# GpSimd gathers the random key columns of every tile but the first; the engine orders are rewritten

## The chip, the cores and the metric

The kernel runs on one core of one Trainium2 chip. The metric is device time in microseconds of one launch; the median of three runs of the kernel before is 801.58 us (798.22 to 808.25). Engines are named PE (TensorE, matmul), DVE (VectorE), ACT (ScalarE), POOL (GpSimd) and SP (the queue that issues most of the DMAs).

## The reference: block-sparse attention, then a cosine feed-forward

```python
B, H, S, D = 4, 8, 768, 64; block = 32          # 24 blocks of keys and of queries
scores = q @ k.transpose(0, 1, 3, 2) / sqrt(D)
mask = |blk_i - blk_j| <= 1, or blk_i or blk_j is the first or the last block
mask[qb, kb] = True for the 3 random kb in sampled_blocks[qb]   # the same for all batches and heads
attn = softmax(where(mask, scores, -1e9)) @ v
x = attn as (B * S, H * D) = (3072, 512)
h = x @ w_in                                     # 512 -> 2048
out = (h * cos(h)) @ w_out                       # 2048 -> 512
```

All inputs are float32. The kernel splits every operand of a matmul into two float16 parts, high and low, and multiplies three of the four pairs, so each product of the reference is three matmuls.

## The kernel before: 24 tiles, one table of places

The 3072 rows are 24 tiles of 128 query rows, six in each of the four batches. The first five of a batch (i = 0 to 4) are sparse: four query blocks each, whose keys are their neighbours, the first and the last block, and three random blocks for each query block. The sixth is dense under a mask. Two tiles make one block of the feed-forward, m0 to m11.

**Names of steps.** For a sparse tile n: wgd and wga gather its random key columns; qk{n}_0 to qk{n}_3 are the scores of two heads each; mx adds the mask and takes row maxima; ex exponentiates; ph and pl split the probabilities; PT turns them by a DMA; pv{n}_0 to pv{n}_3 multiply with the values; no, xh, xl and xT normalise, split and turn the rows for the feed-forward. A feed-forward block m has 16 up steps m{m}_p_c (12 matmuls each) and 16 down steps d{m}_p_t_h (6 matmuls each). vi{n}_0 to vi{n}_3 are indirect DMAs of POOL that fetch the random value rows of tile n. kT turns the keys of a batch into the buffer W, by DMA.

**The gather.** W holds a batch's keys with the key index in the free dimension. The 12 random blocks of a tile are copied into Wg, 8 heads of 32 columns for each copy, at offsets that stand in registers. There is one buffer Wg, so the gather of tile n + 1 can't start before the last score step of tile n has read it, and the first score step of tile n + 1 needs it. In batch 0, tiles 1 to 4 are gathered by POOL (wgp, line 1564, 12 copies). Tile 0 and all tiles of batches 1 to 3 are gathered by DVE (8 copies) and ACT (4 copies) side by side (line 1434), with a tile i = 0 of a later batch in two halves, as soon as each half of W is there. The registers are loaded by load_pool_regs on POOL (12 each for i = 1 to 4, at the start, line 1207) and by load_regs on DVE (8 each) and ACT (4 each) for i = 0 to 4 (line 1217); those of i = 1 to 4 come later, between other work.

**Other single buffers.** The scores of a step lie in sp, of which there is one: a score step waits until mx of the step before has read sp. V, the values of a tile, has two buffers, and POOL's vi steps of a tile wait for one to come free.

**The order.** All steps are named and listed once. The string PLACES gives each a place, and every engine runs its steps in the order of places; the costs in the code (the numbers after the engine in op(...)) only choose which buffer of a class a step takes. So the order on each engine, on SP's and POOL's queues too, is what PLACES says.

```python
    def k_gather(self, n, Wg, h0, h1, which):
...
            src = Wz[:, h0:h1, :, bass.ds(reg, BLK // 2)]
            dst = Wg[:, h0:h1, j, BLK * s : BLK * s + BLK].rearrange("p h (z c) -> p h z c", z=2)
            if which == 2:
                self.nc.gpsimd.tensor_copy(dst, src)
            else:
                self.copy(dst, src, which)
```

Of the kernel before, what the change touches and what calls it, by code (L numbers as in the profile page):

```python
# [45 lines left out]
    GP=[0, 1, 1, 1, 1],  # L46
# [37 lines left out]
wlm5 344 wlp5 345 wc11_2 346 wl14 347 wl15 348 xl0 349 mx2_3_0 350 mx2_3_1 351 pv1_0 352 pv1_2 353 PF2_0_1 354 nb2_3 355 wlp4 356 wc13_0 357 wc13_1
358 ph2_0_0 359 ph2_0_1 360 pl2_0_1 361 ex2_3_0 362 ph1_3_0 363 ex2_2_0 364 ph1_3_1 365 wgp3 366 qk3_0 367 mx3_0_0 368 mx3_0_1 369 qlo4 370 qk3_1 371
ql5 372 ql5#2 373 uT4 374 nb3_0 375 ex3_0_0 376 ex3_0_1 377 ph3_0 378 pl1_3_0 379 wlm7 380 wlp7 381 pl1_3_1 382 pl2_0_0 383 wc13_2 384 wsq13 385 wl16
386 wl17 387 pl3_0 388 mx3_1_0 389 mx3_1_1 390 nb3_1 391 wlm6 392 wc14_0 393 wc15_0 394 wc14_1 395 wc15_1 396 wc14_2 397 wl18 398 wc15_2 399 wl19 400
wlp6 401 PF2_1_0 402 PF2_1_1 403 pv1_1 404 qk3_2 405 mx3_2_0 406 mx3_2_1 407 PF2_2_0 408 PF2_2_1 409 pv1_3 410 no1 411 ex2_3_1 412 qsq5 413 vg4_0 414
vg4_1 415 vi4_0 416 vi4_2 417 vi4_3 418 ex3_1_0 419 wsq9 420 wsq11 421 wred8 422 ph2_1_0 423 pl2_1_0 424 ph2_1_1 425 ex3_1_1 426 ph3_1 427 wall8s 428
wall8 429 wsc8c 430 wsq15 431 wred12 432 wsc8e 433 nb3_2 434 ph2_2_0 435 pl2_2_0 436 ph2_2_1 437 XF1 438 xh1 439 qk3_3 440 pv2_0 441 wsc8s 442 whi8  # L90
443 wsi8 444 wlm8 445 wlm9 446 wlp8 447 wc17_0 448 qsc5c 449 whi10 450 rs2 451 PF2_3_1 452 mx3_3_0 453 mx3_3_1 454 pl2_1_1 455 pv2_1 456 qsc5e 457
pl2_2_1 458 pv2_2 459 wall12s 460 nb3_3 461 ex3_3_1 462 pl3_1 463 PT3_1 464 ex3_2_0 465 wlm10 466 wc17_1 467 wc17_2 468 wl20 469 wl21 470 vg4_2 471
wall12 472 PF2_3_0 473 wgp4 474 qk4_0 475 turn0_1 476 wsc12c 477 xl1 478 vi4_1 479 wsc12e 480 m0_0_0 481 m0_0_1 482 wc18_0 483 wc19_0 484 wc18_1 485
wlp9 486 qu5 487 wc19_1 488 PT3_0 489 ex3_3_0 490 ph2_3_0 491 ph2_3_1 492 pl2_3_1 493 wc19_2 494 wl23 495 mx4_0_0 496 wlp10 497 ph3_3 498 m0_0_2 499
m0_0_3 500 mx4_0_1 501 ex3_2_1 502 ph3_2 503 rs3 504 pl3_2 505 ev0_0_0 506 ev0_0_1 507 pl2_3_0 508 pv2_3 509 nb4_0 510 ex4_0_0 511 rr3 512 wc18_2 513
# [387 lines left out]
def plan_kernel(env, B, H, S, D, DM, DFF, pr):  # L483

    pl = Plan()
    e = env
    NB = S // BLK
    NT = S // P
# [62 lines left out]
    for which in range(2):  # L551
        for i in range(pr["RN"][which]):
            load_regs(i, which)
# [1495 lines left out]
```

## Time and profile before

| what | value |
|---|---|
| median of 3 runs | 801.58 us (798.22 to 808.25) |
| the profiled execution: its own time, its span | 804.44 us, 802.5 us |
| busy: PE, DVE, ACT, POOL | 730.0, 636.2, 624.3, 133.0 us |
| granted TensorE clock, mean over the span | 0.968 |
| chain that ended last, by engine | PE 50%, DVE 21%, DMA 10%, ACT 10% |

Busy time is the sum of an engine's instructions; a PE that is busy is not PE at its peak. The chain is followed back from the last instruction, at each step to what released it. The profiled execution's own time is 2.9 us above the median of the runs.

### The profile page before, as it was taken

Reading aid. Unit: us, or ns where it says so; the run is one execution under the profiler, and the core shown is the slowest. Engines: PE = TensorE matmul, PEld = TensorE weight load, DVE = VectorE, ACT = ScalarE, POOL = GpSimd, SP = SyncE. Lnnn points to the kernel's source line nnn. Section 1 sums busy time; section 2 is a strip of 40 time slices with the busy share of each in tenths; the row PEclk is TensorE's granted clock in tenths of the full one; section 3 lists DMA queues with packets and bytes.
Section 4 is the critical chain, followed back from the end, with each engine's and each line's share of the span. In section 5 each row is a group of like instructions: output and inputs, shape, how many; then the busy total and the mean of one; then the engine's idle time right before and its main releaser. Section 6 shows DMA issues by size and latency. Waiting matters only on the chain.

```text
span 802.5 us, 25057 instructions
## 1 busy us (share of the span) xinstructions
PE 730.0 (91%) x10288; PEld 486.7 (61%) x10288; DVE 636.2 (79%) x1576; ACT 624.3 (78%) x1202; POOL 133.0 (17%) x180
## 2 busy tenths in 40 slices
PE   3587799986999888999999999999799999999998
PEld 3445475654675546756666557677466577566763
DVE  4979999999789875988868988988588858876362
ACT  2578889897669986989969989898589976896242
POOL 1667440002100221001110223001202202000000
PEclk9679999998999979999999999999999999999999
DMA  9885798999746999999998899999848979664101
GB/s 240 275 251 150 219 230 199 202 201 228 179 95 117 173 187 175 192 228 224 182 184 148 167 216 212 180 196 227 187 71 159 156 137 173 155 136 92 28 1 52
DMA packets 295410, 136.97 MB, mean 171 GB/s; under 512 B 253952, under 2 KB 275584, under 8 KB 295296
## 3 DMA queue, kind: packets, MB, share of 16 engines
q1 hardware_dynamic: 290176, 119.65, 73.2%
q0 software_dynamic: 5120, 15.73, 8.4%
q8 instruction: 80, 1.31, 0.7%
q14 instruction: 34, 0.28, 0.1%
HBM read 68.23 MB, written 12.58 MB: 101 GB/s over the span
## 4 chain that ended last, share of the span: by engine, by line
PE 50%; DVE 21%; DMA 10%; ACT 10%; issue 5%; POOL 2%; SPq 1%; ACTq 0%; DVEq 0%; POOLq 0%
PE ph L1920 22%; PE ph L1970 17%; DVE P L1625 4%; DMA PT<-ring 4%; ACT P L1646 3%; DMA xT<-n 3%; DVE ring L1660 2%; PE sp L1590 2%; PE ph L1708 2%; DMA qs<-in_q_dram 2%; PE sp L1609 1%; PE ph L1724 1%; POOL Wg L1564 1%; ACT junk L1302 1%; PE ph L1696 1%
## 5 line engine op out<-in xcount | busy, mean ns | idle before, releaser
L1920 PE MATMUL ph<-xT,w 128*128 128x256 f16 x2304 | 269.6, 275 | 11.1 <-DMA xT<-n 11.1
L1970 PE MATMUL ph<-w,g 128*128 128x512 f16 x1152 | 266.3, 381 | 2.1 <-DVE ot L1747 1.1
L1920 PEld LDWEIGHTS <-w 128*128 128x128 f16 x2304 | 223.4, 99 | 48.2 <-DMA xT<-n 10.5
L1970 PEld LDWEIGHTS <-g 128*128 128x128 f16 x1152 | 107.6, 98 | 121.9 <-issue 6.0
L1549 POOL DMA_INDIRECT V<-scr,gidx x80 | 90.9, 1136 | 508.6 <-PE ph L1696 255.8
L1646 ACT ACTIVATE P<-P,sm 128x352 f32<-128x352 f32 (+1 forms) x224 | 152.1, 680 | 17.2 <-DVE sm L1640 14.8
L1625 DVE CUSTOM_DVE_ANT_1 P<-sp,bias 128x352 f32<-128x352 f32 x160 | 77.4, 518 | 31.5 <-PE sp L1595 26.1
L1660 DVE TENSOR_TENSOR ring<-P,ring 128x704 f16<-128x704 f32 (+1 forms) x100 | 90.2, 909 | 14.9 <-ACT ring L1656 14.7
L1929 ACT ACTIVATE hs<-ph,sm 128x512 f32<-128x512 f32 x96 | 63.0, 677 | 28.9 <-PE ph L1920 25.7
L1656 ACT CAST ring<-P 128x704 f16<-128x704 f32 (+1 forms) x100 | 78.6, 789 | 7.4 <-DMA PT<-ring 6.1
L1947 ACT ACTIVATE g<-g,sm 128x1024 f32<-128x1024 f32 x48 | 54.8, 1146 | 25.8 <-DVE g L1943 25.4
L1952 DVE SCALAR_TENSOR_TENSOR hs<-hs,sm,g 128x1024 f32<-128x1024 f32 x48 | 61.3, 1280 | 14.7 <-ACT g L1947 14.6
L1961 DVE TENSOR_TENSOR g<-hs,g 128x1024 f16<-128x1024 f32 x48 | 58.5, 1220 | 14.8 <-ACT g L1958 14.7
L1958 ACT ACTIVATE g<-hs 128x1024 f16<-128x1024 f32 x48 | 50.4, 1051 | 20.0 <-DVE hs L1952 17.7
L1943 DVE SCALAR_TENSOR_TENSOR g<-g,hs 128x1024 f32<-128x1024 f32 x48 | 58.7, 1224 | 1.2
L1939 DVE TENSOR_SCALAR g<-hs 128x1024 f32<-128x1024 f32 x48 | 33.0, 687 | 26.1 <-ACT hs L1929 26.0
L1590 PE MATMUL sp<-W,U 64*128 64x192 f16 x960 | 43.3, 226 | 11.0 <-DVE sm L1625 10.9
L1590 PEld LDWEIGHTS <-U 64*128 64x128 f16 x960 | 30.0, 98 | 33.2 <-issue 31.5
L1708 PE MATMUL ph<-V,PT 128*128 128x64 f16 x960 | 42.5, 195 | 0.0
L1646 ACT ACTIVATION_READ_ACCUMULATOR P<-P,sm 128x1 f32 x224 | 42.3, 189 | 0.0
L1625 DVE CUSTOM_DVE_ANT_1 P<-sp,dbias 128x384 f32<-128x384 f32 x64 | 33.1, 552 | 5.1 <-PE sp L1609 3.9
L1595 PE MATMUL sp<-Wg,U 64*32 64x96 f16 x1920 | 29.3, 212 | 8.3 <-POOL Wg L1564 4.2
(163 smaller groups left out, 868.0 us busy)
## 6 DMA issues: line engine op xcount, KB each, us to landing
V<-scr SPq DMA_DIRECT2D x20, 384.0 KB, 5.0
w<-in_moe_w_in_dram SPq DMA_DIRECT2D x12, 512.0 KB, 5.8
w<-in_moe_w_out_dram SPq DMA_DIRECT2D x12, 512.0 KB, 4.7
V<-scr SPq DMA_DIRECT2D x8, 768.0 KB, 5.6
scr<-n SPq DMA_DIRECT2D x21, 256.0 KB, 3.3
qs<-in_q_dram SPq DMA_DIRECT2D x20, 256.0 KB, 4.3
stage<-in_v_dram SPq DMA_DIRECT2D x9, 512.0 KB, 5.8
stage<-in_k_dram SPq DMA_DIRECT2D x9, 512.0 KB, 5.6
```

The lines of the kernel that those rows point to most:

```text
L1549: self.nc.gpsimd.indirect_dma_start(V[:96, 2 + j, :], None, self.scr[b][:, :], bass.IndirectOffsetOnAxis(ap=self.gidx[:96, c : c + 1], axi ...
L1590: mm(out, u[r], x, start=(first and not part), stop=False, tile_position=(a * D, 0))
L1625: self.nc.vector.tensor_tensor_reduce(out=self.p_view(n, Pt)[:, a].rearrange("p (n c) -> p n c", c=hf), in0=sp[:, :w].rearrange("p (n c) - ...
L1646: self.nc.scalar.activation(Pv[:, a], Pv[:, a], AF.Exp, scale=qc[:, 4:5], bias=nb[:, a : a + 1], accum_out=sums[:, x : x + 1],)
L1656: self.nc.scalar.copy(R[:, :, 0, : self.width(n)], self.p_view(n, Pt))
L1660: self.nc.vector.tensor_tensor(R[:, :, 1, :w], self.p_view(n, Pt), R[:, :, 0, :w], ALU.subtract)
L1708: mm(xp[:, h, :], PT[:, 6 * a + 3 * l + c, :], V[:, c, h, d0:d1], start=False, stop=(a == 1 and c == 1 and x == len(terms) - 1),)
L1920: self.nc.tensor.matmul(ph[:, ff, :], self.W1[p][:, wl, cc, c * P : (c + 1) * P], xT[:, xl * NCC + cc, :], start=(j == 0), stop=(j == len( ...
L1929: self.nc.scalar.activation(hs[:, h * 512 : h * 512 + 512], ph.rearrange("p f t -> p (f t)"), AF.Copy, scale=self.turns[b][:, p : p + 1])
L1943: self.nc.vector.scalar_tensor_tensor(kt, kt, MAGIC, hs, op0=ALU.subtract, op1=ALU.subtract)
L1952: self.nc.vector.scalar_tensor_tensor(hs, hs, c[:, p : p + 1], kt, op0=ALU.mult, op1=ALU.mult)
L1970: self.nc.tensor.matmul(self.flat32(po), g[:, gl, ff, t * P : (t + 1) * P], self.W2[p][:, wl, ff, :], start=(first and ff == half * hf and ...
```

## The change

POOL gathers the keys of all tiles but the first, in batches 1 to 3 too (12 copies for each tile, for i = 0 in two halves of 12). DVE and ACT gather tile 0 alone, and their register loads for i = 1 to 4 go. POOL loads the registers of i = 1 to 3 once at the start, as before; those of i = 0 and i = 4 it loads each time, in the instructions just ahead of the copies. The table PLACES is new as a whole, and a few costs in the code. The diff without the table:

```diff
-    for i in range(1, NS):
+    for i in range(1, NS - 1):
         if pr["GP"][i]:
             pregs[i] = Val()
             op("POOL", 3.2, pr["RG"][i], lambda i=i: e.load_pool_regs(i), r=[sx], w=[pregs[i]], name=f"pregs{i}")
     for which in range(2):
         for i in range(pr["RN"][which]):
-            load_regs(i, which)
+            if not pr["GP"][i]:
+                load_regs(i, which)
...
-        if i in pregs and not b:
+        if b:
+            for h0, h1 in [(0, HH), (HH, H)] if i == 0 else [(0, H)]:
...
+                cost = (7.1 if h1 - h0 == H else 5.1) + (0.0 if i in pregs else 3.2)
+                op("POOL", cost, pos + 0.01 * h0, lambda h0=h0, h1=h1: e.k_gather(n, Wg.t, h0, h1, 2), r=part + [pregs.get(i, sx)], w=keys, name=f"wgp{n}")
+            return
+        if pr["GP"][i] and not b:
...
-            op("POOL", 4.6, pos, lambda: e.k_gather(n, Wg.t, 0, H, 2), r=part + [pregs[i]], w=keys, name=f"wgp{n}")
+            op("POOL", 7.1 if i in pregs else 10.3, pos, lambda: e.k_gather(n, Wg.t, 0, H, 2), r=part + [pregs.get(i, sx)], w=keys, name=f"wgp{n}")
...
-        for k, reg in enumerate(self.pregs[i] if which == 2 else self.regs[i, which]):
+        for k, reg in enumerate(self.pool_regs(i) if which == 2 else self.regs[i, which]):
```

In the rows below, line numbers of the changed kernel are 11 higher than those of the kernel before from the changed register functions on (1564 becomes 1575).

On POOL's queue, around the gather of tile 1 (V_107 and V_108 are the two buffers V, the DMA rows are vi steps, and each copy has an ISA row ahead of it). Before:

```order
L1298 TENSOR_SCALAR dbias<-V_107 128x24
L1549 DMA V_107<-scr_124,gidx 96x1024 x4
L1564 ISA
L1564 COPY Wg_109<-W 128x8x32
...
L1549 DMA V_108<-scr_124,gidx 96x1024 x4
```

Now:

```order
L1309 TENSOR_SCALAR dbias<-V_107 128x24
L1560 DMA V_108<-scr_124,gidx 96x1024 x2
L1575 ISA
L1575 COPY Wg_109<-W 128x8x32
...
L1560 DMA V_108<-scr_124,gidx 96x1024 x2
L1560 DMA V_107<-scr_124,gidx 96x1024 x4
```

Two of tile 0's four value fetches have moved behind the copies of tile 1's gather.

On DVE, at the last maxima of tile 8 and the first of tile 9 (the two ISA rows on line 1625 are mx, L1660 is pl, L1961 is a step of the feed-forward). Before:

```order
L1625 ISA P_99,sm<-sp_117,bias 128x352
L1625 ISA sm 128x1
L1217 TENSOR_LOAD sx
L1625 ISA P_99,sm<-sp_117,bias 128x352
L1625 ISA sm 128x1
L1640 TENSOR_SCALAR sm<-sm 128x2
L1434 ISA
L1434 COPY Wg_109<-W 128x8x32
...
L1660 TENSOR_TENSOR ring_103<-P_98,ring_103 128x2x352
L1961 TENSOR_TENSOR g_85<-hs_84,g_85 128x1024
```

Now:

```order
L1636 ISA P_100,sm<-sp_117,bias 128x352
L1636 ISA sm 128x1
L1636 ISA P_100,sm<-sp_117,bias 128x352
L1636 ISA sm 128x1
L1963 SCALAR_TENSOR_TENSOR hs_83<-hs_83,sm,g_88 128x1024
L1671 TENSOR_TENSOR ring_103<-P_99,ring_103 128x2x352
L1518 TENSOR_SCALAR sm<-sm 128x1
L1651 TENSOR_SCALAR sm<-sm 128x2
L1972 TENSOR_TENSOR g_88<-hs_83,g_88 128x1024
```

The register load between the two maxima and the eight copies are gone.

On PE, from the last value step of tile 17 to the first up step of m8, which needs tile 17's turned rows (each row stands for a run of equal ones; L1970 are down steps, L1920 up steps). Before:

```order
L1724 MATMUL ph_118<-V_107,PT_106 128x64
...
L1970 MATMUL ph_122<-w_0_68,g_86 128x512
...
L1970 MATMUL ph_119<-w_0_68,g_86 128x512
...
L1970 MATMUL ph_119<-w_1_69,g_87 128x512
...
L1920 MATMUL ph_121<-xT_110,w_0_64 128x256
```

Now:

```order
L1735 MATMUL ph_122<-V_107,PT_104 128x64
...
L1931 MATMUL ph_123<-xT_111,w_3_67 128x256
...
L1981 MATMUL ph_120<-w_3_71,g_88 128x512
...
L1981 MATMUL ph_122<-w_0_68,g_86 128x512
...
L1931 MATMUL ph_119<-xT_110,w_0_64 128x256
```

Before there are five down steps between the two; now there are two up steps of m7 and seven down steps.

## Rows read from the trace of the kernel before

**Rows 1.** Busy time by stretch: stretch, us, engines, PE clock, DMA share, GB/s.

```profile
160.00:200.00 40.00, 29.54 (x317) 19.89 (x316) 39.55 (x74) 33.47 (x61) 4.62 (x4) 0.93 1.03 216
...
200.00:300.00 100.00, 93.03 (x1298) 59.84 (x1298) 83.44 (x235) 79.32 (x161) 14.24 (x12) 0.94 0.77 151
...
sum 602.50, PE 576.60 PEld 382.61 DVE 456.44 ACT 472.61 POOL 65.37; mean PE 96.10 PEld 63.77 DVE 76.07 ACT 78.77 POOL 10.90
```

**Rows 2.** Groups by line and shape: busy us, mean ns | idle before.

```profile
L1434 DVE COPY Wg<-W 128x256 f16 x104 | 15.4, 223 | 0.2 <-PE sp L1595 0.2
L1434 DVE COPY Wg<-W 128x128 f16 x48 | 5.7, 188 | 1.7 <-DMA W<-kn 1.7
L1434 ACT COPY Wg<-W 128x256 f16 x52 | 17.0, 399 | 0.0
L1434 ACT COPY Wg<-W 128x128 f16 x24 | 5.3, 290 | 1.0 <-DMA W<-kn 1.0
```

**Rows 3.** Register loads by line: duration ns min/median/max.

```profile
L1217 DVEq TENSOR_LOAD <-sx x5: 1847/2096/3264, 9.9 to 286.9; - x5
L1207 POOLq TENSOR_LOAD <-sx x4: 2722/2726/2931, 9.9 to 18.5; - x4
```

**Rows 4.** Timeline of POOL: start, us, [idle before <-releaser].

```profile
46.23 0.92 POOL L1549 DMA_INDIRECT V<-scr,gidx  x1 [0.30 <-DVE sm L1625]
47.16 5.24 POOL L1564 COPY Wg<-W 128x256 f16 x12
...
74.86 7.61 POOL L1564 COPY Wg<-W 128x256 f16 x12 [2.15 <-PE sp L1595]
```

**Rows 5.** The tile Wg: POOL's copies, ns min/median/max.

```profile
L1564 POOL COPY Wg<-W x48: 386/393/1466, 47.2 to 102.7; 128x256 f16 x48
```

**Rows 6.** Timeline of DVE.

```profile
52.83 0.52 DVE L1625 CUSTOM_DVE_ANT_1 P<-sp,bias 128x352 f32<-128x352 f32 x1 [3.18 <-PE sp L1595]
...
80.57 1.29 DVE L1804 SCALAR_TENSOR_TENSOR w<-w,w 128x1024 int32<-128x1024 int32 x1
...
289.96 0.52 DVE L1625 CUSTOM_DVE_ANT_1 P<-sp,bias 128x352 f32<-128x352 f32 x1 [2.56 <-issue]
```

**Rows 7.** Timeline of PE.

```profile
43.35 0.44 PE L1595 MATMUL sp<-Wg,U 64*32 64x96 f16 x24
...
279.45 0.64 PE L1590 MATMUL sp<-W,U 64*128 64x192 f16 x12 [1.71 <-DVE sm L1625]
...
307.31 2.96 PE L1920 MATMUL ph<-xT,w 128*128 128x256 f16 x13 [3.12 <-DMA xT<-n]
...
407.55 4.65 PE L1920 MATMUL ph<-xT,w 128*128 128x256 f16 x41 [0.68 <-DMA xT<-n]
...
573.97 3.21 PE L1920 MATMUL ph<-xT,w 128*128 128x256 f16 x16 [5.58 <-DMA xT<-n]
...
619.30 0.51 PE L1590 MATMUL sp<-W,U 64*128 64x192 f16 x12
619.74 0.32 PE L1595 MATMUL sp<-Wg,U 64*32 64x96 f16 x24
619.99 0.36 PE L1696 MATMUL ph<-V,PT 96*32 96x64 f16 x24
...
620.64 4.09 PE L1920 MATMUL ph<-xT,w 128*128 128x256 f16 x36
...
642.65 1.47 PE L1920 MATMUL ph<-xT,w 128*128 128x256 f16 x12 [1.74 <-DMA xT<-n]
```

**Rows 8.** The chain that ended last: start, us, what.

```profile
266.37 1.02 issue
...
287.40 2.56 issue
...
763.71 9.17 PE ph L1920 x84
...
778.07 20.73 PE ph L1970 x96
```

More of the change, by code (lines that the diff above doesn't have):

```diff
@@ new lines @@
+qlo12 1468 PT10_0 1469 vg10_1 1470 xT8 1471 st2_0 1472 ex11_0_0 1473 pv9_3 1474 kload2_0 1475 PT10_2 1476 no9 1477 st1_1 1478 ph10_3 1479 ex11_1_1
+1480 ka3_2 1481 d3_0_1_0 1482 d3_0_1_1 1483 d3_1_1_0 1484 d3_1_1_1 1485 xh9 1486 pl10_3 1487 vhi2_2 1488 uT12 1489 ex11_0_1 1490 ph11_0 1491 ev3_3_0
+1492 xl9 1493 qk11_3 1494 mx11_3_0 1495 xT9 1496 ex11_1_0 1497 ph11_1 1498 ev3_3_1 1499 kb3_2 1500 vg11_0 1501 pv10_0 1502 vhi2_3 1503 rs10 1504
+mx11_3_1 1505 nb11_3 1506 pl11_0 1507 ka3_3 1508 vlo2_2 1509 PT10_3 1510 ksq2_1 1511 vst2_2 1512 rr10 1513 vhi2_0 1514 vlo2_3 1515 kload2_2 1516
@@ new lines @@
+m5_1_1 1806 ev5_1_0 1807 qk12_3 1808 mx12_3_0 1809 mx12_3_1 1810 nb12_3 1811 m5_1_3 1812 ex12_2_1 1813 ph12_2 1814 ql17 1815 ql17#2 1816 st3_1 1817
+pl12_2 1818 PT12_2 1819 ph12_1 1820 pl12_1 1821 PT12_1 1822 vg13_2 1823 m5_2_2 1824 m5_2_1 1825 vsq3_5 1826 ev5_1_1 1827 ka5_1 1828 kb5_1 1829
+d5_0_0_0 1830 pv12_0 1831 vsq3_2 1832 d4_3_1_0 1833 uT14 1834 ex12_3_1 1835 ex12_3_0 1836 ph12_3 1837 rs12 1838 pl12_3 1839 rr12 1840 PT12_3 1841
+wgp13 1842 qk13_0 1843 mx13_0_0 1844 mx13_0_1 1845 nb13_0 1846 m5_2_3 1847 vsq3_3 1848 qsq17 1849 qsc17c 1850 qsc17e 1851 qsc17s 1852 qu17 1853 qnu17
@@ new lines @@
+ex16_0_1 2097 ex16_1_0 2098 nb16_2 2099 ph16_0 2100 m6_1_3 2101 m6_1_1 2102 qhi18 2103 qlo18 2104 ex16_1_1 2105 pl16_0 2106 m6_2_2 2107 sin6_0 2108
+gm6_0 2109 qk16_3 2110 mx16_3_0 2111 mx16_3_1 2112 nb16_3 2113 ev6_1_0 2114 ev6_1_1 2115 ka6_1 2116 kb6_1 2117 ql19 2118 pv15_3 2119 vg16_0 2120
+vg16_1 2121 vg16_2 2122 vi16_0 2123 vi16_1 2124 vi16_2 2125 vi16_3 2126 m6_2_0 2127 ph16_1 2128 pl16_1 2129 PT16_1 2130 qk17_0 2131 mx17_0_0 2132
+mx17_0_1 2133 gh6_0 2134 gl6_0 2135 pv15_1 2136 m6_2_1 2137 sin6_1 2138 gm6_1 2139 m6_2_3 2140 qk17_1 2141 mx17_1_0 2142 mx17_1_1 2143 nb17_1 2144
@@ new lines @@
+2964 mx23_7_0 2965 mx23_7_1 2966 nb23_7 2967 ex23_6_0 2968 ex23_6_1 2969 ex23_7_0 2970 ex23_7_1 2971 rs23 2972 rr23 2973 pv23_1 2974 pv23_2 2975
+ka10_1 2976 kb10_1 2977 sin10_0 2978 gm10_0 2979 PT23_5 2980 ph23_4 2981 pl23_4 2982 d9_3_0_0 2983 d9_3_0_1 2984 o9_0 2985 m10_2_0 2986 sin10_1 2987
+gm10_1 2988 ph23_6 2989 pl23_6 2990 m10_2_2 2991 ph23_7 2992 pl23_7 2993 gh10_0 2994 gl10_0 2995 m10_2_1 2996 ev10_2_0 2997 pv23_3 2998 m10_3_2 2999
+m10_3_3 3000 m10_2_3 3001 ev10_2_1 3002 ka10_2 3003 kb10_2 3004 d10_0_1_0 3005 gh10_1 3006 gl10_1 3007 PT23_4 3008 pv23_4 3009 d10_0_1_1 3010
@@ L309 @@
+3102 gh11_3 3103 gl11_3 3104 d11_1_0_0 3105 d11_1_1_0 3106 d11_1_1_1 3107 d11_2_1_0 3108 d11_2_1_1 3109 d11_1_0_1 3110 d11_2_0_0 3111 d11_3_1_0 3112
+d11_3_1_1 3113 o11_1 3114 st11_1 3115 st11_1#2 3116 d11_2_0_1 3117 d11_3_0_0 3118 d11_3_0_1 3119 o11_0 3120 st11_0 3121
 """
@@ L682, in prep_q @@
             tp = Val(pr["UC"])
-            op("PE", 0.58, pos, lambda: e.q_turn(qs.t, tp.t), r=[qs, wide], w=[tp], name=f"UF{n}")
+            op("PE", 0.7, pos, lambda: e.q_turn(qs.t, tp.t), r=[qs, wide], w=[tp], name=f"UF{n}")
             op("ACT", 0.613, pos, lambda: e.q_square(qc.t, qs.t, None), r=[qs], w=[am], name=f"qsq{n}")
@@ L729, in gather_k @@
         tiles[n]["Wg"] = Wg
-        if i in pregs and not b:
+        if b:
+            for h0, h1 in [(0, HH), (HH, H)] if i == 0 else [(0, H)]:
+                part = [(W, (h, t)) for h in range(2) if h0 <= h * HH < h1 for t in range(NT)]
+                keys = [(Wg, (x, h)) for x in "da" for h in range(2) if h0 <= h * HH < h1]
+                cost = (7.1 if h1 - h0 == H else 5.1) + (0.0 if i in pregs else 3.2)
+                op("POOL", cost, pos + 0.01 * h0, lambda h0=h0, h1=h1: e.k_gather(n, Wg.t, h0, h1, 2), r=part + [pregs.get(i, sx)], w=keys, name=f"wgp{n}")
+            return
+        if pr["GP"][i] and not b:
             part = [(W, (h, t)) for h in range(2) for t in range(NT)]
             keys = [(Wg, (x, h)) for x in "da" for h in range(2)]
-            op("POOL", 4.6, pos, lambda: e.k_gather(n, Wg.t, 0, H, 2), r=part + [pregs[i]], w=keys, name=f"wgp{n}")
+            op("POOL", 7.1 if i in pregs else 10.3, pos, lambda: e.k_gather(n, Wg.t, 0, H, 2), r=part + [pregs.get(i, sx)], w=keys, name=f"wgp{n}")
             return
@@ L1015, in plan_kernel @@
         for i in range(pr["RN"][which], NS):
-            load_regs(i, which, [by[("ksc0s", "ksq0_2")[which]]])
+            if not pr["GP"][i]:
+                load_regs(i, which, [by[("ksc0s", "ksq0_2")[which]]])
     load_v(0, pr["V0"])
@@ L1203, in const_regs, with pool_regs @@
         nc.vector.memset(self.halfpi, math.pi / 2)
-    def load_pool_regs(self, i):
+    def pool_regs(self, i):
+        if i in self.pregs:
+            return self.pregs[i]
         x = 3 * (1 + 4 * i)
-        self.pregs[i] = self.nc.values_load_multi_w_load_instructions(
+        return self.nc.values_load_multi_w_load_instructions(
             self.sx[0:1, x : x + 12],
@@ L1213, in load_pool_regs @@
         )[1]
+    def load_pool_regs(self, i):
+        self.pregs[i] = self.pool_regs(i)
     def load_regs(self, i, which):
```

479 lines of the change are left out of this document (229 added, 250 removed).

## The prediction

> **What bounds the kernel now.** I read the busy time by stretch first. From 200 us to the end PE is busy 576.6 of 602.5 us, so 25.9 us are left there, and a granted clock of 0.94 in the first of these stretches [rows 1] takes about 6 us more (6% of 100). Before 200 us DVE is the bound: 39.55 of 40 us in the stretch from 160 [rows 1]. DVE and ACT have room behind 200 us (456 and 473 of 602 us), so work taken from them there counts only where PE waits for them. Then I read the timeline of PE for its waits. The long ones behind 200 us are not for a gather: they are for turned rows (3.12, 0.68, 5.58 and 1.74 us) and for mx, which frees the single score buffer (1.71 us) [rows 7]. The chain adds two waits called issue, of 1.02 and 2.56 us, at 266 and 287 [rows 8]; there DVE loads registers between two maxima, and the second is the idle time before the maximum at 289.96 [rows 6, 8].
>
> A step's price on PE, from its pace: an up step 9.17 / 7 = 1.31 us, a down step 20.73 / 16 = 1.30 us [rows 8], a score step 0.69 us (619.30 to 619.99), of which the first 0.44 don't touch Wg, and a value step 0.65 us (to 620.64) [rows 7].
>
> **The change part by part.** Removed: 96 of the 104 full copies on DVE (15.4 x 96/104 = 14.2 us) and the 48 half ones (5.7 us), 48 of 52 and 24 on ACT (15.7 + 5.3 us) [rows 2], together 19.9 us of DVE and 21.0 us of ACT, and four register loads on each (2.1 us on DVE as a median [rows 3]).
>
> *What that gives back.* Nearly all of it lies where PE is the bound and other work covers it. The waits listed above take 12.8 of PE's 25.9 idle us, and not for these engines' gathers; of the rest, which is spread over many short waits, I take -1.0 (ends -3.0 and 0). The loads that end on the chain at 266 and 287 are worth up to 1.02 + 2.56 = 3.6 us [rows 8]; behind them the chain goes on to the turned rows that m3 waits for, so some of it may only lengthen that wait. I take -2.5 (ends -3.6 and 0).
>
> *POOL's gather, its length.* Twelve copies took 5.24 us at 47 us and 7.61 us at 75 us [rows 4]; a copy is 0.39 us as a median and 1.47 at the longest [rows 5]. The long one ran beside DVE operations with two operands in SBUF, such as the one of 1.29 us at 80.57 [rows 6]. The feed-forward has operations of that kind, so I take 6.9 us, nearer the upper end.
>
> *Does PE wait for it?* The new order puts more work on PE between the last score step of one tile and the first of the next. Counting steps in the two orders: before tiles 7, 8 and 9 it was 3.25, 3.9 and 3.25 us, now 5.88 (three up, one down, one value), 6.5 (four down, two value) and 5.85 us (three down, three value). Before tiles 13 to 15 and 19 to 22 it is now 7.15 to 11.1 us, and 10.5 to 11.1 for i = 4 (tiles 10, 16, 22), which also has a load of 2.72 us [rows 3] ahead of its copies. The need is the gather less about 0.4 us, for the part of a score step that doesn't touch Wg: 6.5 us, and 9.2 with the load. So tiles 7 and 9 wait 0.6 and 0.65 us and the others nothing: +1.3. With 5.24 us it is 0, with 7.61 us (need 7.2) 1.3 + 0.7 + 1.35 + 0.1 = +3.5.
>
> *First tiles of a batch.* Two halves, each with a load of 2.72 us and 12 copies of half the size. No such copy is in the trace; the half copy takes 188 for 223 ns on DVE and 290 for 399 on ACT [rows 2], so 3.8 to 5.2 us for twelve, against 0.9 us on DVE and ACT side by side (a sixth of 5.7 and 5.3). The new order has 2.6, 7.0 and 6.5 us more PE work between the maximum of a batch's keys and its first score step (22.2 for 19.6, 35.1 for 28.1, 27.6 for 21.1 us), which covers the difference in batches 2 and 3 and most of it in batch 1: 0, and at most +2 for each of the three batches, if the second half is late.
>
> *Packed scores.* With the work moved between the tiles, less is left between the scores of one tile. In tiles 7 to 9 three pairs of score steps now stand with nothing between them, where it was one pair; that one waited 1.71 us for mx [rows 7]. Two more such waits are 3.4 us; the old order also lost time to mx elsewhere in these tiles, for which I take off one such wait: +1.7 (ends +1.0 and +2.6).
>
> *POOL's queue at the start.* Tile 0's last score step ended at 43.8 us [rows 7], but POOL was still issuing vi until 47.15 and only then gathered tile 1 [rows 4]; DVE sat idle 3.18 us before 52.83 for the scores behind it [rows 6], in the one part where DVE has idle time ahead of the stretch that it bounds. With two vi behind the copies the gather can start up to 3.3 us earlier. The moved vi must land before tile 0's values are multiplied, several us later. The vlo steps that POOL waits for ahead of its first vi now stand behind the first maxima, which gives back a part: -2.5 (ends -3.3 and 0). The four scores of tile 0 are packed too, +-2 around zero. The load of i = 4 that leaves the start had no one waiting.
>
> *Turned rows.* PE work between a tile pair's last value step and the first up step: for m5 10.4 us, now 7.8; m6 12.6, now 8.2; m8 6.5, now 11.7; m9 7.2, now 6.6; m3 7.4, now 8.7; m11 9.1, now 7.8; the rest hardly change or have more. What was needed is the old work plus the wait [rows 7]: m5 11.1, m8 12.1, m9 8.9 us. So m8 gives back 5.2 of its 5.58 us; m5 loses 2.6, m9 0.6; m6, whose need I put between 8.9 and 12.3 us, loses 2.4 (0.7 to 4.1); m11 0.6; m3 gives back 1.3. Sum -0.3 (ends -4.5 and +3.5).
>
> **Sum:** -1.0 - 2.5 + 1.3 + 0 + 1.7 - 2.5 + 0 - 0.3 = -3.3 us. On the profiled execution's 804.44 us that is 801.1; the median stands 2.9 us below that execution, so 798.3 us. Ends added up: -15.4 and +17.6 us.
>
> **A rule that speaks against it.** In the trace the copies beside large two-operand work on DVE reach 1.47 us where 0.39 is usual [rows 5]. The Trainium skill, page SBUF — State Buffer, section SBUF: two separate sides, says that VectorE and GpSimd share a pair of ports under an exclusive lock, and that the one that comes second is blocked for the whole of the other's instruction, also by a VectorE instruction with two inputs in SBUF. By this trace the rule holds for the length of a stretched copy; taken to its end it is the first rival.
>
> **The rivals.** (1) *Slower: the gather becomes the bound.* If DVE puts a two-operand instruction of 1.29 us between any two copies, twelve copies take 12 x (0.39 + 1.29) = 20 us. For it: copies of 1.47 us exist. Against it: the worst of the old gathers, beside weight conversion, took 7.61 us [rows 4]. The waits add up, over the twelve full gathers, to 1.3 us at 6.9, 22 us at 10 and about 32 us at 11. The sum changes its sign from 7.8 us on, and passes 2% from 9.8 on; at 11 the time is 798.3 - 1.3 + 32 = 829 us. (2) *The new order misplaces the transposes.* m5, m6, m9 and m11 at their upper ends (2.6 + 4.1 + 0.6 + 1.3), m8 and m3 giving nothing back: +8.6 for -0.3, so 807 us, within 2%. For it: the order counts on landing times, and 5.58 us at m8 shows how it can miss. (3) *Faster: relief on DVE and ACT frees PE.* Of the 25.9 + 6 us that idle time and the lower clock cost behind 200 us [rows 1], half goes: 798.3 - 16 = 782 us. Against it: the longest waits are for DMAs, which the change doesn't shorten. (4) *The registers aren't ready:* the loads don't run ahead while POOL waits, and stand in front of the copies for i = 4 and i = 0; for i = 4 10.5 us of PE work cover it, at a batch's start the one between the two halves stays, three times 2.72 us [rows 3]: +8, so 806 us, within 2%.
>
> **How the numbers follow.** 2% of 801.6 is 16 us, which is about what a measurement of this kernel tells from no change. Forecast (798.3, its own range 788 to 808) 0.58; rival 2 0.15, rival 4 0.09, rival 3 0.10, rival 1 0.08. Faster by over 2% is rival 3, 0.10; slower is rival 1, 0.08; the rest, 0.82, within 2%. The range leaves out most of rivals 1 and 3: 786 to 812 us.
>
> **What the changed profile would show.** POOL's copies for twelve full gathers of 6 to 8 us; PE waits on Wg of under 1.5 us, at tiles 7 and 9; tile 1's gather starting near 44 us; no load on DVE between maxima; m8 with a wait below 1 us for its turned rows and m5 and m6 with 2 to 4 us. I am wrong if gathers take 10 us, if the first 200 us move by more than 4 us either way, or if a new wait of several us stands at a batch's first scores.

## The result and the profile after

The kernel after takes 798.72 us (median of 20 runs, 792.63 to 808.17); the kernel before, run beside it, 805.9 us (20 runs, 798.22 to 811.36). The ratio is 0.9905, with a 95% interval of 0.9879 to 0.9930: 1% faster, 5.6 to 9.8 us, which is within the 2%. In every ratio of this document executions over 1.5% above the fastest of the same kernel are left out as slow (the profiles of e6 and e11 are of such executions), so a ratio can differ from that of the two medians. The profiled execution took 799.69 us for a span of 797.9 us, 4.75 us less than that of before.

The busy time by stretch of the kernel after, and the first stretch of the kernel before; the columns are those of [rows 1], and the sum is over the whole execution:

```profile
0.00:205.00 205.00, 164.18 (x2400) 111.31 (x2400) 185.76 (x475) 159.65 (x320) 66.74 (x125) 0.91 0.89 219
...
sum 900.00, PE 730.83 PEld 485.03 DVE 629.10 ACT 605.57 POOL 236.66; mean PE 91.35 PEld 60.63 DVE 78.64 ACT 75.70 POOL 29.58
```

```profile
0.00:205.00 205.00, 158.36 (x2328) 108.32 (x2329) 183.27 (x472) 153.81 (x311) 67.64 (x124) 0.92 0.88 218
```

Up to 205 us PE stands idle 40.8 us; before it was busy 158.36 us there and idle 46.6. Behind 205 us it is idle 592.9 - 566.65 = 26.3 us of the 592.9 that are left, for 25.9 of 597.5 before. PE's whole busy time has stayed (730.8 for 730.0 us). So in this pair of executions the time came out of the first 205 us, and behind them waits went and others came.

Which these are stands in the view of PE's waits, of the kernel after: what PE waited for, us in all, times, longest.

```profile
PE sp L1601 <- DVE sm L1636: 14.4, 14, 2.3
...
PE ph L1931 <- DMA xT<-n: 4.6, 3, 2.5
PE sp L1606 <- POOL Wg L1575: 4.3, 5, 1.5
...
PE ph L1707 <- DMA V<-scr,gidx: 2.7, 1, 2.7
...
PE ph L1707 <- DMA PT<-ring: 2.2, 2, 1.6
```

The same view of the kernel before:

```profile
PE ph L1920 <- DMA xT<-n: 11.1, 4, 5.6
PE sp L1590 <- DVE sm L1625: 10.9, 11, 2.3
...
PE ph L1347 <- DVE sm L1333: 8.3, 4, 2.8
PE ph L1724 <- DMA PT<-ring: 6.3, 3, 5.1
```

It also has 4.2 us for POOL's gather and 3.8 for that of DVE and ACT (0.9 now), nothing for V, and 3.0 us more for turned probabilities (PT) in a second group. Turned rows and turned probabilities gave back 6.5 and 7.1 us; mx and V took 3.5 and 2.7. Other waits went both ways: those for the maxima of keys, values and weights (line 1333, now 1344) fell from 8.3 to 3.7 us, and those for DVE's normalised rows (ot) and its part of the feed-forward (g) rose from 1.6 to 6.6.

POOL's timeline after, for the gathers of tiles 1, 7, 8 and 14, which answer to [rows 4]:

```profile
42.01 6.52 POOL L1575 COPY Wg<-W 128x256 f16 x12
...
251.96 8.00 POOL L1575 COPY Wg<-W 128x256 f16 x12 [5.32 <-PE sp L1606]
...
266.48 4.83 POOL L1575 COPY Wg<-W 128x256 f16 x12 [6.52 <-PE sp L1606]
...
435.99 9.87 POOL L1575 COPY Wg<-W 128x256 f16 x12 [6.76 <-PE sp L1606]
```

The gather of tile 1 starts 5.15 us earlier than it did. The twelve full gathers of batches 1 to 3 take 4.83 to 9.87 us, 6.8 in the mean. The six halves take 3.20 to 5.77 us, and nobody waits for them.

PE's timeline after, at the places that the prediction named and at tile 14 (answering to [rows 7]):

```profile
260.02 0.30 PE L1606 MATMUL sp<-Wg,U 64*32 64x96 f16 x18 [1.54 <-POOL Wg L1575]
...
398.68 3.60 PE L1931 MATMUL ph<-xT,w 128*128 128x256 f16 x18 [2.53 <-DMA xT<-n]
...
445.91 0.28 PE L1606 MATMUL sp<-Wg,U 64*32 64x96 f16 x17 [1.51 <-POOL Wg L1575]
...
474.88 1.36 PE L1931 MATMUL ph<-xT,w 128*128 128x256 f16 x11 [1.60 <-DMA xT<-n]
...
572.15 4.09 PE L1931 MATMUL ph<-xT,w 128*128 128x256 f16 x36
```

The first and the third row are tiles 7 and 14 waiting for POOL; m5 and m6 wait for turned rows; m8, the last row, has no wait in brackets at all, where it had 5.58 us [rows 7]. On DVE one register load is left, at the start (line, engine, operation: ns, first and last start):

```profile
L1228 DVEq TENSOR_LOAD <-sx x1: 2093/2093/2093, 8.1 to 8.1; - x1
```

### The profile page after: what moved, and what is told of

It is laid out like the page before. It is cut to its first block, busy times and chain, and to the rows that moved or that the text cites. A ratio compares the mean times of both kernels' runs of the same rounds, so it can differ in the third digit from the quotient of the medians.

```text
span 797.9 us, 25126 instructions
## 1 busy us (share of the span) xinstructions
PE 730.8 (92%) x10288; PEld 485.0 (61%) x10288; DVE 629.1 (79%) x1432; ACT 605.6 (76%) x1130; POOL 236.7 (30%) x396
## 3 DMA queue, kind: packets, MB, share of 16 engines
q8 instruction: 80, 1.31, 0.7%
## 4 chain that ended last, share of the span: by engine, by line
PE 46%; DVE 20%; ACT 13%; DMA 11%; issue 6%; POOL 3%; SPq 1%; POOLq 0%; DVEq 0%; ACTq 0%
PE ph L1931 18%; PE ph L1981 16%; DMA PT<-ring 4%; ACT P L1657 3%; DVE P L1636 3%; POOL Wg L1575 3%; PE sp L1601 2%; PE ph L1719 2%; DVE hs L1963 2%; DVE g L1954 2%; PE sp L1606 2%; DVE ring L1671 1%; DMA xT<-n 1%; PE ph L1707 1%; DMA stage<-in_k_dram 1%
## 5 line engine op out<-in xcount | busy, mean ns | idle before, releaser
L1981 PE MATMUL ph<-w,g 128*128 128x512 f16 x1152 | 270.2, 384 | 4.6 <-DVE g L1972 3.1
L1575 POOL COPY Wg<-W 128x256 f16 (+1 forms) x264 | 134.9, 561 | 141.9 <-PE sp L1606 95.2
L1560 POOL DMA_INDIRECT V<-scr,gidx x80 | 86.3, 1078 | 270.6 <-PE ph L1735 102.9
L1671 DVE TENSOR_TENSOR ring<-P,ring 128x704 f16<-128x704 f32 (+1 forms) x100 | 92.4, 931 | 18.3 <-ACT ring L1667 17.8
L1958 ACT ACTIVATE g<-g,sm 128x1024 f32<-128x1024 f32 x48 | 54.8, 1147 | 21.8 <-DVE g L1954 21.4
```

What stands on the lines that cost most here:

```text
L1560: self.nc.gpsimd.indirect_dma_start(V[:96, 2 + j, :], None, self.scr[b][:, :], bass.IndirectOffsetOnAxis(ap=self.gidx[:96, c : c + 1], axi ...
L1671: self.nc.vector.tensor_tensor(R[:, :, 1, :w], self.p_view(n, Pt), R[:, :, 0, :w], ALU.subtract)
L1981: self.nc.tensor.matmul(self.flat32(po), g[:, gl, ff, t * P : (t + 1) * P], self.W2[p][:, wl, ff, :], start=(first and ff == half * hf and ...
```

## The experiments

The runs were made on three chips, each time beside the kernel before. It takes 831.86 us on the first chip (e1 to e4), 830.43 on the second (e5 to e7 and the kernel after again) and 806.11 on the third (e8 to e11); the last section comes back to that. Which chip the pair of kernels above ran on is not on record; by its time it is like the third.

### Each half of the change alone

The gather on POOL in the order of before (e1), every pair in the table replaced by POOL's step:

```diff
-wgd7 ... wga7
+wgp7
```

> The order of before on every engine, but POOL gathers tiles 6 to 10, 12 to 16 and 18 to 22, at the places where DVE and ACT did, and the loads of registers go. Theory A (the gather moved by itself costs time, because it takes 6.9 us for about 3 and the new order is there to cover it): counted in the order of before, PE has 3.3 to 4.1 us of work between the tiles at 7, 8, 9, 13, 15 and 19 and 4.7 to 6.7 at 10 and 16, where the gather needs 6.5 (9.2 with a load), so PE waits up to 23 us more on Wg; some of that is taken off other waits, and 3.5 us of relief: 10 to 20 us slower than before, ratio 1.012 to 1.025. Theory B (DVE and ACT relief is the gain, the order is not needed): no longer than the kernel after, ratio 0.99 to 0.995.

Measured: 853.6 us for 831.86, ratio 1.0259 (1.0209 to 1.0310). The view of PE's waits of e1:

```profile
PE sp L1589 <- DVE sm L1624: 19.4, 14, 3.5
PE sp L1594 <- POOL Wg L1563: 12.8, 17, 1.6
```

The gather moved by itself costs 2.6%, 22 us, a little over the 20 of theory A, and theory B is out: in the old order the relief of DVE and ACT does not pay for the waits that come with it. How much it gives by itself, e1 does not separate. Where the 22 us go can be read beside e7 (below), the kernel before less its register loads, on the second chip; the spans of the two traces are 27.6 us apart. PE's waits on Wg, for all three engines, are 16.7 us in e1 and 5.6 in e7. And behind 205 us the same 8046 matmuls keep PE busy for 598.1 us in e1 and 580.4 in e7, at a mean granted clock of 0.96 and 0.98. So in this pair the waits on Wg are less than half of the price, and PE's slower pace is most of the rest. DVE also has 38.2 us of the stops that the last section tells of in e1 and 21.7 in e7; whether the price is the same on the third chip, which lacks them, was not tried.

The new order with the gathers on DVE and ACT again (e2), in the places of POOL's steps:

```diff
-wgp7
+wgd7 wga7
```

> The new order on every engine, but DVE and ACT gather as in the kernel before, at the places where POOL does after, with their loads of registers behind the same steps as before. Theory A (the gain is in the new order, most of it in the first 205 us, where PE stands idle 5.9 us less in the trace after; the gather itself gives 3.5 us of relief at most): ratio 0.991 to 0.997, the first 205 us as after. Theory B (relief is the gain): 0.998 to 1.005.

Measured: 861.51 us, ratio 1.0356 (1.0307 to 1.0405). Neither theory had that. PE's waits in e2:

```profile
PE sp L1582 <- DVE Wg L1421: 15.6, 19, 3.8
PE ph L1957 <- ACT g L1945: 11.0, 2, 10.3
```

A place that suits POOL is wrong for DVE and ACT: late in their queues PE waits for the copies (15.6 us), and early, at tile 6, ACT stands still 5.68 us until 259.06 in front of copies whose keys haven't landed, and PE waits 10.33 us for the step behind them. So a second try (e5) put each pair behind the last maximum of the tile before, where Wg is free for DVE:

```diff
-wgp9
+mx8_3_1 wgd9 wga9
```

> The new order with the gathers of DVE and ACT again, but now each stands right behind the last maximum of the tile before, where Wg is free, and those of tiles 6 and 18 close to their first score step, so that no gather stands late in front of PE's scores or early in front of DVE's and ACT's other work. Theory A (order alone carries the gain): 0.985 to 0.994, as fast as after or faster. Theory D (the order pays only with DVE and ACT free of gathers and loads, since it packs the scores of a tile): 0.997 to 1.010.

Measured: 851.93 us for 830.43, ratio 1.0276 (1.0238 to 1.0313). ACT's timeline of e5, at the gather of tile 9:

```profile
301.45 1.32 ACT L1421 COPY Wg<-W 128x256 f16 x4 [11.02 <-PE sp L1582]
```

PE waits 5.1 us for DVE's copies now, but ACT, whose exponentials stand later in the new order, stood still 11.02 us for tile 8's last score step, with those exponentials behind it. A stop of DVE of 4.48 us, of the kind that the last section tells of, lies within these 11.02. Neither range holds 1.0276; theory D has the direction: the new order doesn't go with gathers in these queues as I placed them. Whether a table made for them could do as well is open. On POOL a step that waits holds up nothing but vi.

### Where in the run the gain is

The new order up to tile 5's last value step, and the order of before behind it with its gathers and loads (e3); and the reverse (e4), both cut at pv5_7:

```diff
-order of before
+order of after up to pv5_7, then what is left in the order of before
```

> The new order up to the last value step of tile 5 (about 204 us), and behind it the order of before for all that is left, with the gathers of DVE and ACT and their loads. Theory A (the gain lies in the first 205 us): 5 to 6 us faster than before, ratio 0.992 to 0.995, and the idle time of PE before 205 us is near 41 us (46.7 before). Theory C (the gain lies behind 205 us, in the gather, the loads and the turned rows, as the prediction's sum has it, -0.8 us in the first 205 us and more behind): 0.997 to 1.001.

> The order of before up to the last value step of tile 5, and behind it the new order with the gathers of POOL. Theory A: what stands behind 205 us gives nothing, ratio 0.997 to 1.002. Theory C: this is where the gain is, 0.990 to 0.994, with the new order of the start worth nothing.

Measured: e3 826.76 us, ratio 0.9942 (0.9907 to 0.9977); e4 826.89 us, ratio 0.9957 (0.9924 to 0.9989), both to 831.86 us. The two parts add up to -1.0%, which is the whole change. Theory A has the start right; that the rest gives nothing is wrong: it gives 0.9 to 6.3 us. So both parts gain, the start 1.9 to 7.7 us. Up to 205 us PE stands idle 45.5 us in e3 and 52.0 in e4, on the same chip: not the 41 that theory A named, but a difference like that between after and before (5.8).

A part of what the start gains is seen at tile 5's values. PE's timelines, first of e4 (old start):

```profile
205.85 2.00 PE L1723 MATMUL ph<-V,PT 128*128 128x64 f16 x36 [3.22 <-DMA PT<-ring]
```

and of e3 (new start):

```profile
201.11 1.80 PE L1711 MATMUL ph<-V,PT 128*128 128x64 f16 x54
...
214.35 1.22 PE L1711 MATMUL ph<-V,PT 128*128 128x64 f16 x36 [0.98 <-DMA PT<-ring]
```

In the kernel before the same wait was 5.08 us (PE's timeline, then SP's):

```profile
196.16 2.10 PE L1724 MATMUL ph<-V,PT 128*128 128x64 f16 x36 [5.08 <-DMA PT<-ring]
```

```profile
186.00 6.90 SPq L1686 DMA_TRANSPOSE PT<-ring  x2
```

In SP's queue the transpose that it is for (PT5_4) went out last of this pair, which took SP until 192.90 us, behind two weight loads, the rows of tile 8 and PT5_7. In the new order it goes out at 184.72, ahead of one of the weight loads, these rows and PT5_7 (SP's timeline after):

```profile
184.72 1.68 SPq L1697 DMA_TRANSPOSE PT<-ring  x1
186.45 0.75 SPq L1805 DMA_DIRECT2D g<-in_moe_w_out_dram  x1
187.25 0.44 SPq L1493 DMA_DIRECT2D qs<-in_q_dram  x1
187.74 4.46 SPq L1535 DMA_TRANSPOSE U<-n  x1
192.36 1.27 SPq L1697 DMA_TRANSPOSE PT<-ring  x1
```

The wait went with the new start in all traces: at tile 5's values PE waits 2.4 to 5.8 us for PT in the five traces with the old start (before, e1, e4, e7, e10) and 0 to 1.9 us in the nine with the new one. That SP's queue alone did it is not shown. The order on DVE changed too: the split that PT5_4 sends out (pl5_4) stood behind that of PT5_7 and ended at 187.19 us before; now it stands ahead of it and ends at 184.65, just before PT5_4 goes out. The two were not tried apart.

### The kernel after on a slower chip, and the value fetches

The kernel after again (a_after), without an edit:

> The kernel after again, on the chip of the other runs of this call, as their measure. The parts measured so far (new start -0.6%, new rest with the gather -0.4%) add up to a ratio of 0.990, and it was 0.9905. If these parts are real and not of one chip: 0.987 to 0.994. If they depend on the chip, elsewhere.

Measured: 823.4 us for 830.43, ratio 0.9904 (0.9868 to 0.9940). The gain is there on this chip too.

The two value fetches back ahead of tile 1's gather (e6):

```diff
-vi0_2 vi0_3 wgp1 ... vi0_1 ... vi0_0
+vi0_0 vi0_1 vi0_2 vi0_3 wgp1
```

> The kernel after with the two value fetches vi0_0 and vi0_1 back ahead of tile 1's gather on POOL. My prediction's term (the gather of tile 1 earlier gives 2.5 us, and the moved fetches land in time): 2 to 3 us slower than after. Rival from the trace after (PE waits 2.7 us for V at tile 0's values at 56 us, and DVE has no need of the earlier gather): 1 to 3 us faster than after.

Measured: 822.35 us, ratio 0.9885 (0.9843 to 0.9927) for 0.9904: not slower by what could be seen, and the two theories lie too close together for these intervals (1.6 us faster than after, with 4.6 either way). What the traces say stands at the term on POOL's queue below.

### The register loads

The kernel before without the loads for i = 1 to 4 on DVE and ACT (e7):

```diff
     def load_regs(self, i, which):
+        if i:
+            self.regs[i, which] = self.regs[0, which]
+            return
```

> The kernel before without the eight register loads of DVE and ACT for i = 1 to 4: their tiles use the registers of i = 0, so that the same copies are made from other blocks, and the outputs of these tiles are of other keys. My term of the prediction: 2.5 us faster than before (0 to 3.6), ratio 0.997. Rival (the chain goes on to the turned rows that m3 waits for, and the loads are worth nothing): 0 us, ratio 1.000, with m3's wait longer by what the loads gave.

Measured: 827.38 us for 830.43, ratio 0.9963 (0.9932 to 0.9994): 3.05 us, and 0.5 to 5.6 by the interval. That is the term of the prediction, and not the rival's zero. With the loads, on the first chip, e3's DVE has this at the place of [rows 6]:

```profile
275.07 0.53 DVE L1612 CUSTOM_DVE_ANT_1 P<-sp,bias 128x352 f32<-128x352 f32 x1 [3.51 <-issue]
```

In the trace of e7 no maximum between 275 and 300 us waits for issue.

### The price of the gather

One copy of twelve (e8) and eighteen copies for twelve (e9), in batches 1 to 3:

```diff
+        ks = list(enumerate(self.pool_regs(i) if which == 2 else self.regs[i, which]))
+        if which == 2 and self.seq[n][0]:
+            ks = ks[:1]          # e9: ks + ks[:6]
-        for k, reg in enumerate(self.pool_regs(i) if which == 2 else self.regs[i, which]):
+        for k, reg in ks:
```

> The kernel after with one of the twelve copies of each POOL gather in batches 1 to 3 (the other eleven blocks of Wg stay as the tile before left them, so the outputs of these tiles are of other keys). My term for PE's waits on the gather is 1.3 us, and the trace after shows 3.6 us of them behind 200 us: 2 to 4 us faster than after, ratio 0.985 to 0.988. Rival (the copies also slow DVE's work, so that all 104 us that POOL copies after 200 us cost something): 10 us faster than after or more, 0.978 or less.

> The kernel after with eighteen copies for twelve in each POOL gather of batches 1 to 3 (the first six are made twice): a full gather of about 10.4 us for 6.9. This prices my first rival. By the covers that I counted between the tiles (5.9 to 8.7 us, 10.7 to 11.3 for i = 4) and a need of 10.0 us (12.7 with a load), PE waits 29.6 us: 26 us more than after, ratio 1.015 to 1.026. Rival (the waits for mx, turned rows and V take most of it up): 5 to 10 us more than after, ratio 0.996 to 1.003.

Measured, to 806.11 us: e8 796.88 us, ratio 0.9886 (0.9842 to 0.9930); e9 822.22 us, ratio 1.0192 (1.0144 to 1.0239). By the ratios e8 is 1.5 us faster than after, with 4.1 either way, and the rival's 0.978 is outside: the copies cost what PE waits for them and nothing more that shows in the time. DVE is busy for 434.7 us behind 205 us in e8, for 443.3 in the kernel after and 444.0 in e9: its operations may be a little longer beside the copies, where PE is the bound. e9 is 23 us slower than after (4.3 either way), near the 26 expected, though PE's waits on Wg are 21.4 us in all and not 29.6. PE's waits in e9, and POOL's longest and shortest full gather there (tiles 14 and 10):

```profile
PE sp L1597 <- POOL Wg L1566: 21.4, 17, 2.7
```

```profile
302.55 7.08 POOL L1566 COPY Wg<-W 128x256 f16 x18 [4.65 <-PE sp L1597]
...
441.84 11.93 POOL L1566 COPY Wg<-W 128x256 f16 x18 [6.53 <-PE sp L1597]
```

At tile 14 the need (the gather less 0.4 us) is 11.93 - 0.4 us, the cover (PE's work ahead of it) 7.97, so 3.6 us should be missing; PE waited 2.70 and 0.81 us. At tile 13 it is 9.68 - 0.4 - 7.25 = 2.0, and 1.06 and 0.81 were waited.

### The turned rows

One edit of the order of before, the cover of m8 (e10):

```diff
-m7_3_2 m7_3_3 d6_3_1_0 d6_3_1_1 pv17_5 pv17_6 pv17_7
+pv17_5 pv17_6 pv17_7 m7_3_2 d6_3_1_0 d6_3_1_1 m7_3_3
```

> The order of before with one edit: the four steps m7_3_2, d6_3_1_0, d6_3_1_1 and m7_3_3 stand behind tile 17's last value step instead of ahead of its last three, so that PE has 11.7 us of work instead of 6.5 ahead of m8. My term (m8 gives back 5.2 us by its cover): 4 to 6 us faster than before, ratio 0.993 to 0.995. Rival (tile 17's transposes land only just in time for its value steps, 558.8 us for the last issue and 561 for the last value step, so that these wait instead, and the turned rows come no sooner): 0 to 1 us, ratio 0.998 to 1.001, with a wait of 3 to 5 us for PT at tile 17.

Measured: 807.5 us for 806.11, ratio 1.0026 (0.9994 to 1.0058). The rival is right. PE's timeline of e10, and SP's:

```profile
561.64 3.12 PE L1711 MATMUL ph<-V,PT 128*128 128x64 f16 x54 [4.34 <-DMA PT<-ring]
...
577.45 4.75 PE L1907 MATMUL ph<-xT,w 128*128 128x256 f16 x42
```

```profile
552.64 8.53 SPq L1673 DMA_TRANSPOSE PT<-ring  x3
```

m8 waits no longer, but tile 17's values wait 4.34 us for transposes that SP issued until 561.2 us. The four steps had hidden that wait; put elsewhere, they hide the other one. In the kernel after SP has issued the last of tile 17's transposes by 555.15 us, in before by 558.77, and there the same cover does give back the 5.58 us.

Three edits of the kernel after, meant to beat it (e11):

```diff
-vi0_2 vi0_3 wgp1 ... vi0_1 ... vi0_0
+vi0_0 vi0_1 vi0_2 vi0_3 wgp1
-kT2_0_0 kT2_0_1 PT11_6 kT2_0_2 PT11_7
+PT11_6 PT11_7 kT2_0_0 kT2_0_1 kT2_0_2
-d4_0_1_0 d4_0_1_1 pv11_6 pv11_7
+pv11_6 pv11_7 d4_0_1_0 d4_0_1_1
```

> The kernel after with three edits: vi0_0 and vi0_1 back ahead of tile 1's gather; tile 11's last two transposes ahead of three of the keys' on SP's queue; the down steps d4_0_1_0 and d4_0_1_1 behind tile 11's last value step, where they cover m5's wait for turned rows (2.5 us in the trace after, 2.8 in that of this chip). If the waits add up: 2 to 4 us faster than after, ratio 0.985 to 0.988. If the transposes don't land sooner, m5's wait moves to tile 11's value steps: as after, 0.988 to 0.992.

Measured: 804.28 us, ratio 0.9919 (0.9878 to 0.9959, from seven of the twelve executions), as the kernel after. In its trace m5 still waits 3.40 us. DVE's and SP's timelines of e11:

```profile
398.16 0.69 DVE L1750 TENSOR_TENSOR n<-ot,n 128x512 f16<-128x512 f32 x1
```

```profile
399.89 4.14 SPq L1763 DMA_TRANSPOSE xT<-n  x1
```

The value steps were done at 392.79 us, but DVE came to xl, the split of these rows, only at 398.16, behind work that I hadn't moved: 5.4 us after the values, where it was 2.6 in the kernel after (388.38 to 390.99). The wait moved to a third queue.

## Why the prediction was right, and where its steps were wrong

The forecast was no measurable change by 2%, 798.3 us; it is that. The sum is too small: -3.3 us, where 5.6 to 9.8 were measured. That 798.3 came so close to 798.72 is luck: the median of three runs that it started from lay 4.3 us below that of twenty.

**POOL's queue at the start (-2.5): not borne out.** The gather of tile 1 did start earlier, by more than I said. The step that failed is "the moved vi must land before tile 0's values are multiplied, several us later". Of PE's timeline after:

```profile
59.28 0.36 PE L1707 MATMUL ph<-V,PT 96*32 96x64 f16 x24 [2.73 <-DMA V<-scr,gidx]
```

Here they landed 2.73 us too late. In e8, with the same start, the wait is 0.79 us, and in e9 and in the kernel after on the second chip there is none: the margin is about nothing, and not several us. Nor does the earlier gather show. In e11, where the fetches stand ahead again, the step starts at 59.35 us without such a wait, and in the kernel before at 59.31; e6 was not slower. Tile 5's first score step starts at 135.9 us before (136.2 in e10), at 135.1 after (132.7 in e8, 133.3 in e9) and at 133.9 in e11: by then the new start has given some 1 to 3 us, with the fetches on either side of the gather. On the first two chips even that is not clear (144.9 to 146.4 us for 145.8 to 148.6).

**Tile 5's transposes: missing (about -5 in this pair, -2.2 from e4 to e3).** It is the largest single wait that went, and no term had it. I read that DVE bounds the stretch from 160 us, and left PE's waits there alone; DVE is as busy there after (39.65 of 40 us) as before [rows 1], and still a PT wait of 5.08 us went with the order on SP's and DVE's queues. I had listed PE's waits only from 200 us on. My own sign for a wrong prediction, the first 200 us moving by over 4 us, came true.

**Register loads (-2.5): right.** -3.05 us by e7 (0.5 to 5.6), and no load stands between maxima any more.

**Relief of DVE and ACT (-1.0): not seen, so at its upper end of 0.** PE's waits for DVE's and ACT's own gathers fell by 2.9 us, but 2.7 of that is at tile 0, which the two still gather. Behind 205 us the kernel before lost 0.3 us to them.

**Gather and waits (+1.3): right in its rule, low in its size.** The mean of 6.8 us is the 6.9 taken. The waits came at tiles 7, 14 and 15 (1.54, 1.51 and 0.56 us, 3.6 in all, just over the upper end of 3.5), since single gathers lie between 4.83 and 9.87 us. A value step takes 0.74 us there (257.06 to 257.80), not the 0.65 that I priced, so the covers are a little longer than I counted; the need less the cover is 8.00 - 0.4 - 5.96 = 1.64 at tile 7, 9.87 - 0.4 - 7.97 = 1.5 at tile 14. At tile 9 PE should have waited 1.15 us and did not: it had stood 1.62 us for turned probabilities, at 287.09. The price of a mean is not the mean of the prices where only the long ones show. On the spread, the Trainium skill's rule (SBUF — State Buffer, section SBUF: two separate sides), by which VectorE and GpSimd keep each other out of a shared port, agrees in direction with gathers that vary by a factor of two for the same twelve copies; which of DVE's operations stretched which copy was not tried.

**First tiles (0): right.** No wait on the halves, which took 3.20 to 5.77 us.

**Packed scores (+1.7): right in sign, low.** Tiles 7 to 9 wait 5.6 us for mx after (1.15, 0.43, 1.15, 0.46, 1.98, 0.41), 3.7 before (0.67, 1.71, 1.31): +1.9. Over the whole kernel mx takes 3.5 us more.

**Turned rows (-0.3): signs right for m8, m3, m5 and m6, size wrong.** It gave -6.5 us by the two views of waits. m8 gave 5.58 and m3 3.12 (I had 1.3 for m3), m9 1.3 where I had a loss of 0.6; m5 lost 1.9 and m6 1.6 (2.6 and 2.4 predicted), m11 nothing. The rule behind it, that what is needed is the old cover plus the wait, takes the turned rows to be as late after the values as before, and the values to be ready. e10 shows that it isn't so by itself: the same cover in the old order gave nothing, because the transposes ahead were late. That m8's 5.2 us came true needed SP's new order too, which my sum left out. And not all of the 5.58 us is a gain: ahead of m8, at 566.97, PE now waits 1.50 us for ACT. I also passed over m1 and m2, whose cover fell by 2.6 and 3.9 us; neither waits.

**The rivals.** (1) The gather as the bound is priced by e9: 23 us more at a mean of 9.7 us (twelve full gathers), for my 22 at 10; the length was not reached. My 22 counts no load ahead of the tiles i = 4, with which it would be 27; (4) shows that leaving it out was right. (2) Not seen as a whole; m5 and m6 are its part, and smaller. (3) e1 speaks against it as a whole, and e8 shows that POOL's copies did not hide it. (4) Out for i = 4: with a load of 2.72 us [rows 3] behind the wait, the gathers of tiles 10, 16 and 22 would start that much later. In the trace after they start 0.15, 0.17 and 0.17 us after the last score step ahead of them has ended (299.59 us after 299.44 for tile 10), and tile 7's, which has no load, 0.17. So these loads run while POOL waits.

What stays open: which terms make up the rest's gain in e4, on a chip where other waits are long than in the pair above; whether SP's order or DVE's took tile 5's wait away; and what the new order alone is worth with gathers on DVE and ACT that are placed well.

## What to carry to other kernels

Before a cover on the matrix engine is counted as a gain, look at what comes late next in each queue ahead of the wait: e10 and e11 bought cover and only moved the wait, to a transpose in SP's queue and to a split in DVE's. A step moved to an engine that has little else to do could wait in its queue here at no cost but its own lateness (need less cover, gather by gather, gave PE's waits to some 0.2 us in most tiles), and the same step in a full queue blocked what stood behind it (e2, e5). List the waits of the engine that you hope to speed up over the whole span, also where another engine is busy all the time.

## What was not expected of the hardware

On the two chips of the first eight runs the same kernels take 3% longer (831.86 and 830.43 for 806 us before, 823 for 799 after), while single operations take nearly the same time (in e3 the maximum 520 for 518 ns as a mean, an up matmul 277 for 275 ns). The traces from there have stops that those of before, after and e8 to e11 lack. In e3 DVE and ACT stand still for 5.5 us and start again within 0.04 us of each other, and in a_after DVE stops 4.57 us before a maximum whose scores were done 4 us earlier (timelines of DVE and ACT in e3, then of DVE in a_after):

```profile
57.19 0.53 DVE L1612 CUSTOM_DVE_ANT_1 P<-sp,bias 128x352 f32<-128x352 f32 x1 [5.47 <-remote]
57.23 0.59 ACT L1871 CAST w<-ph 128x512 f16<-128x512 f32 x1 [5.52 <-remote]
```

```profile
287.12 0.52 DVE L1636 CUSTOM_DVE_ANT_1 P<-sp,bias 128x352 f32<-128x352 f32 x1 [4.57 <-remote]
```

In e3 DVE has 20.1 us of such waits for maxima, and PE 8.5 us of waits called issue (0.6 in the trace of before). What they wait for the profile doesn't show, and it was not tried. The ratio of after to before was the same on the second chip, 0.9904, as in the pair above, 0.9905.
